# Two MLPs behind a retention attention: weights split in pairs, first weight loaded ahead of the chunks

## The chip, the cores and the metric

The kernel runs on one core of one Trainium2 chip. The metric is the device time of one execution in microseconds (us); less is better. It is the time of the whole program on that core, from the first load to the last store.

## The reference, cut to what matters

Four batches of 576 tokens (2304 in all) with 8 heads of 64 dimensions go through a retention attention, and then through two MLPs of 512 to 2048 to 512 columns, all in float32:

```python
scores = q @ k.T / sqrt(64);  D[i, j] = gamma[h] ** (i - j) if i >= j else 0
x = (scores * D) @ v                                  # per head, heads side by side: 2304 x 512
x = softplus(x @ w1_in) @ w1_out                      # first MLP, softplus = max(h, 0) + log1p(exp(-|h|))
out = relu(x @ w2_in) ** 2 @ w2_out                   # second MLP
```

The weights of both MLPs lie in memory as 64-bit floats, so a row of weights is loaded as pairs of 32-bit words.

## The kernel before

**Precision.** A float32 matrix product is made of three products of reduced-precision float32 (fp32r): each operand is split into a part `hi` (a rounding copy) and a part `lo` (the operand less `hi`), and hi*hi, lo*hi and hi*lo are summed in PSUM.

**Weights.** A weight tile is 128 x 512. `load_w` brings its 64-bit numbers (512 KB) into one of three staging slots (`STAGES = 3`) by the SP queue; the load of a slot's next owner waits until the slot has been read. `words` makes float32 of it: on ACT L140 (`Prelu`) and L141 (`Identity`), on DVE L145 (shift and or), which is the last to read the slot and writes `ct`. Then `split_w` makes `hi` on ACT (L173) and `lo` on DVE (L174). So a weight tile costs three operations of 128 x 512 on ACT and two on DVE. `items` is the order in which weights are split, `pump_step` does one part of the next item, `pump(n)` whole items; `weights(j)` says how many items are to be done by step j. There are 16 tiles of `wi` (first matrix) and 16 of `wo` (second) in each MLP.

**Opening.** The attention works on chunks of 64 tokens. `load_chunk(c)` loads q and k (`qk`, 256 KB) and k and v (`kv`, 256 KB) by SP; `scale_v(c)` (L311) multiplies v by decay factors; `step_s(c)` does 16 or 32 small matmuls (scores L326, state L332), masks the scores on DVE (L336) and copies the state on ACT (L338); `step_o(c)` does 16 matmuls into `po` (L348), makes `x` on DVE (L361), its hi part `xh` on ACT (L365) and its lo part `xl` on DVE (L366). `make_xw` (DVE, L710) prepares factors. The first eight chunks make the first tile of tokens; the code from `with tc.manual_schedule()` on writes the order on every engine by hand. `scale_v` runs there on POOL, but for chunk 7, which is done on DVE. `keep_warm` puts filler matmuls (`cold`, L684) between. `wi` 0 is loaded behind chunk 4, `wi` 1 and 2 behind chunk 7, and from chunk 5 on one `pump_step` follows each chunk.

**First MLP.** Tokens go in five tiles of 512, 384, 512, 512 and 384 (`TILES`), each in 16 steps f. Step j: `g1(j)`, 12 matmuls (L401) into one of two PSUM banks; `softplus_a` on ACT (L415 to L417), `split_g` of the step before (ACT L437, DVE L438); then the weights that are due (first tile only) and attention work for the next tile (`attend`); `g2(j - 2)`, 12 matmuls (L453); `softplus_b` on DVE (L422, L425, L428, which frees the bank). A scheduler decides how these interleave on each engine. The weights of the first MLP stay in SBUF, hence only the first tile splits weights.

**Second MLP.** It works by Strassen-like products (L545, seven for every block) and pieces (L564). Their left operands are sums of weight blocks that `split_s` makes during tiles 1 to 3 and stores in DRAM (`s2d`, read back into `S_SLOTS` slots); the right operands (`build_t`: ACT L533, DVE L534 on 768 columns) are built in the last tile of the first MLP, in buffers that the first MLP's `wi` leaves. The last tile and the first block also split the second MLP's `wo`.

## Time and profile before

| | us |
|---|---|
| median of three executions | 874.39 (874.03 to 876.84) |
| the profiled execution | 873.48 |
| its span, first to last instruction | 871.7 |
| PE busy | 858.3 |
| DVE busy | 579.7 |
| ACT busy | 422.2 |

The profile is of one execution. Its time is 1.78 us above its span (what lies around the first and the last instruction). PE is TensorE's matmuls, PEld its weight loads, DVE is VectorE, ACT is ScalarE, POOL is GpSimd, SP is SyncE, which here only issues DMAs. A row of a timeline gives start, duration, engine, line and operation, `out<-in`, shapes, and in brackets how long the engine had been idle before and what ended that.

### The profile page before, as it was taken

Reading aid. Unit: us, or ns where it says so; the run is one execution under the profiler, and the core shown is the slowest. Engines: PE = TensorE matmul, PEld = TensorE weight load, DVE = VectorE, ACT = ScalarE, POOL = GpSimd, SP = SyncE. Lnnn points to the kernel's source line nnn. Section 1 sums busy time; section 2 is a strip of 40 time slices with the busy share of each in tenths; the row PEclk is TensorE's granted clock in tenths of the full one; section 3 lists DMA queues with packets and bytes.
Section 4 is the critical chain, followed back from the end, with each engine's and each line's share of the span. In section 5 each row is a group of like instructions: output and inputs, shape, how many; then the busy total and the mean of one; then the engine's idle time right before and its main releaser. Section 6 shows DMA issues by size and latency. Waiting matters only on the chain.

```text
span 871.7 us, 14212 instructions
## 1 busy us (share of the span) xinstructions
PE 858.3 (98%) x5520; PEld 754.4 (87%) x5520; DVE 579.7 (67%) x1002; ACT 422.2 (48%) x763; POOL 8.8 (1%) x12
## 2 busy tenths in 40 slices
PE   8899999999999999999999999999999999999998
PEld 7777888999888888888999989888888988998896
DVE  3799899977896578745788874447645446553544
ACT  2599997665675446644696561213322113221121
POOL 2100000000000000000000000000000000000000
PEclk9999999999999999999999999999999999999999
DMA  9867764861583117610432464436644343644442
GB/s 209 229 181 211 220 210 148 246 203 50 165 264 104 30 45 239 221 36 1 170 115 55 149 226 121 120 110 193 193 115 115 121 118 115 191 120 115 116 121 85
DMA packets 75766, 126.32 MB, mean 145 GB/s; under 512 B 6706, under 2 KB 41650, under 8 KB 75698
## 3 DMA queue, kind: packets, MB, share of 16 engines
q1 hardware_dynamic: 75700, 125.42, 48.7%
q8 instruction: 44, 0.72, 0.3%
q14 instruction: 22, 0.18, 0.1%
HBM read 101.28 MB, written 24.12 MB: 144 GB/s over the span
## 4 chain that ended last, share of the span: by engine, by line
PE 83%; DMA 6%; DVE 4%; ACT 4%; issue 1%; SPq 0%; POOL 0%; DVEq 0%; ACTq 0%
PE acc L564 23%; PE acc L453 18%; PE ph L401 18%; PE py L545 9%; PE px L545 6%; PE pz L545 6%; PE st L326 2%; DMA wo_raw<-in_moe_w_out_dram 2%; DMA ch<-in_kv_dram 2%; PE po L348 2%; DMA wi_raw<-in_moe_w_in_dram 1%; DVE ct L145 1%; PE st L332 1%; DMA ch<-in_qk_t_dram 1%; ACT e L416 1%
## 5 line engine op out<-in xcount | busy, mean ns | idle before, releaser
L401 PE MATMUL ph<-xh,wi 128*128 128x512 f32 (+1 forms) x640 | 146.2, 369 | 2.9 <-DVE e L428 2.1
L401 PEld LDWEIGHTS ph<-xh,wi 128*128 128x128 f32 x640 | 116.3, 188 | 19.9 <-DVE e L428 2.2
L453 PE MATMUL acc<-gh,woh 128*128 128x512 f32 (+1 forms) x320 | 120.5, 378 | 0.0
L453 PE MATMUL acc<-gl,woh 128*128 128x512 f32 (+1 forms) x320 | 117.8, 368 | 0.2 <-DVE gl L438 0.2
L453 PE MATMUL acc<-gh,wol 128*128 128x512 f32 (+1 forms) x320 | 117.8, 368 | 0.0
L564 PE MATMUL acc<-woh,gring 128*128 128x512 f32 x288 | 104.9, 393 | 0.0
L545 PE MATMUL py<-t,sring 128*128 128x384 f32 x432 | 86.9, 335 | 0.3 <-DVE uring L652 0.3
L545 PEld LDWEIGHTS py<-t,sring 128*128 128x128 f32 x432 | 77.2, 188 | 6.8 <-DVE uring L652 0.6
L437 ACT CAST gh<-e 128x512 fp32r<-128x512 f32 (+1 forms) x80 | 45.8, 573 | 71.6 <-DVE e L428 54.2
L401 PE MATMUL ph<-xl,wi 128*128 128x512 f32 (+1 forms) x320 | 78.7, 367 | 0.0
L422 DVE SCALAR_TENSOR_TENSOR e<-e 128x512 f32<-128x512 f32 (+1 forms) x80 | 50.9, 636 | 38.0 <-ACT l L417 37.2
L438 DVE TENSOR_TENSOR gl<-e,gh 128x512 fp32r<-128x512 f32 (+1 forms) x80 | 50.9, 636 | 29.1 <-ACT gh L437 28.6
L453 PEld LDWEIGHTS acc<-gh,woh 128*128 128x128 f32 x320 | 60.0, 188 | 8.9 <-ACT gh L437 0.2
L453 PEld LDWEIGHTS acc<-gh,wol 128*128 128x128 f32 x320 | 60.1, 188 | 7.9
L590 ACT CAST gh<-g 128x384 fp32r<-128x384 f32 x48 | 24.6, 513 | 86.8 <-DVE g L577 72.1
L453 PEld LDWEIGHTS acc<-gl,woh 128*128 128x128 f32 x320 | 60.1, 188 | 7.5 <-DVE gl L438 0.4
L401 PEld LDWEIGHTS ph<-xl,wi 128*128 128x128 f32 x320 | 58.7, 188 | 7.6
L590 ACT CAST gring<-g 128x384 fp32r<-128x384 f32 x48 | 24.6, 513 | 83.0 <-DVE g L577 83.0
L415 ACT ACTIVATE e<-ph 128x512 f32<-128x512 f32 (+1 forms) x80 | 44.0, 550 | 37.3 <-PE ph L401 37.1
L564 PEld LDWEIGHTS acc<-woh,gring 128*128 128x128 f32 x288 | 54.0, 188 | 9.2
L545 PE MATMUL px<-t,sring 128*128 128x384 f32 x288 | 58.3, 337 | 0.0
L545 PE MATMUL pz<-t,sring 128*128 128x384 f32 x288 | 58.2, 337 | 0.0
(82 smaller groups left out, 1497.1 us busy)
## 6 DMA issues: line engine op xcount, KB each, us to landing
sring<-s2d SPq DMA_DIRECT2D x168, 256.0 KB, 2.7
wi_raw<-in_moe_w_in_dram SPq DMA_DIRECT2D x32, 512.0 KB, 4.6
wo_raw<-in_moe_w_out_dram SPq DMA_DIRECT2D x32, 512.0 KB, 4.2
s2d<-ct SPq DMA_DIRECT2D x48, 256.0 KB, 3.0
ch<-in_qk_t_dram SPq DMA_DIRECT2D x36, 256.0 KB, 4.3
ch<-in_kv_dram SPq DMA_DIRECT2D x36, 256.0 KB, 4.9
raw<-x2d SPq DMA_DIRECT2D x12, 384.0 KB, 3.3
out_dram<-xo SPq DMA_DIRECT2D x18, 256.0 KB, 2.2
```

The source lines that it names most:

```text
L145: nc.vector.scalar_tensor_tensor(out=ct, in0=up, scalar=3, in1=low, op0=ALU.logical_shift_left, op1=ALU.bitwise_or,)
L326: nc.tensor.matmul(pb[HI, h, :], lhsT=kk[LO, h, :], rhs=qp[LO, h, :], start=True, stop=True, skip_group_check=True,)
L348: nc.tensor.matmul(po[(LO, HI)[h % 2], h // 2, :], lhsT=sv[rows, h, :], rhs=qp[rows, h, :], start=True, stop=True, skip_group_check=True,)
L401: nc.tensor.matmul(ph[:, :n], lhsT=a, rhs=x, start=(j == 0), stop=(j == len(todo) - 1))
L415: nc.scalar.activation(out=e, in_=ph[:, :n], func=AF.Abs)
L422: nc.vector.scalar_tensor_tensor(out=e, in0=e, scalar=-2.0, in1=e, op0=ALU.add, op1=ALU.mult)
L437: nc.scalar.copy(h[:, :n], g)
L438: nc.vector.tensor_tensor(out=l[:, :n], in0=g, in1=h[:, :n], op=ALU.subtract)
L453: nc.tensor.matmul(acc[j][:, :n], lhsT=a, rhs=x, start=(begin and m == 0), stop=(end and m == 2))
L545: nc.tensor.matmul(ps, lhsT=a, rhs=x, start=(first and m == 0), stop=(m == len(todo) - 1), skip_group_check=True,)
L564: nc.tensor.matmul(acc2[j, m], lhsT=a, rhs=x, start=(begin and n == 0), stop=(end and n == 2))
L590: nc.scalar.copy(h, g)
```

## The change

**Pairs.** Weights are split in pairs of tiles. The words of the two tiles are still made one by one (L140, L141, L145), each into one half of a `ct` of 2 x 512 columns; then one ACT copy (L172 of the changed file) and one DVE subtraction (L173) work on 1024 columns. `wi` 0 and `wi` 1 stay single. After each tile's words one further load is asked for. The order of items becomes `wi` 0, `wi` 1, `wi` 2-3, `wo` 0-1, `wi` 4-5, `wo` 2-3 and so on; `weights(j)` counts pairs. `split_s` and the stores of its results use pair buffers too, but keep their operations.

**Buffers.** `cvt` has three slots of 2 x 512 columns in place of six of 512. `wi` tiles lie in groups of six in place of three, `wo` in pairs; `build_t` uses such a group for four results, and runs in steps 7 to 10 and 13 to 15 of the last tile (before: 4, 5, 7, 8, 10, 11, 13), and the last tile splits a pair in steps 4, 7, 10 and 13 (before: one tile in every even step from 4). `S_SLOTS` goes from 5 to 4.

**Opening.** The load of `wi` 0 is the first behind the two rows of constants; one `pump_step` follows each of chunks 0 to 2 (before: 5 to 7). All `scale_v` are on POOL; 12 fillers in place of 4 stand ahead of chunk 0; `make_xw(8)` comes last.

```diff
-EARLY = {"wi": 9, "wo": 8}
-GROUP = 3
+EARLY = {"wi": 12, "wo": 8}
+GROUP = 6
...
-S_SLOTS = 5
+S_SLOTS = 4
...
-    cvt = ctx.enter_context(tc.tile_pool(name="cvt", bufs=6))
+    cvt = ctx.enter_context(tc.tile_pool(name="cvt", bufs=3))
...
-        return cvt.tile([P, DM], dtype, tag="ct", name="ct")
+        return cvt.tile([P, 2, DM], dtype, tag="ct", name="ct")
...
-    def split_w(phase, kind, f):
-
-        t = staged.pop((kind, f))
-        ct = new_ct()
-        yield from words(t, ct)
+    def split_w(i, n, phase, kind, f):
+
+        ct = new_ct()[:, :n]
+        for o in range(n):
+            yield from words(staged.pop(i + o), ct[:, o])
+            pump_load(i + o + 1 + STAGES)
         y = ct.bitcast(F32)
...
+        w = wi_group[phase, kind, g][:, m:m + n]
+        hi, lo = w[:, :, 0], w[:, :, 1]
         nc.scalar.copy(hi, y)
         nc.vector.tensor_tensor(out=lo, in0=y, in1=hi, op=ALU.subtract)
...
+    want(1, split_w, (0, "wi", 0), (w1_in, "wi", 0))
+    want(1, split_w, (0, "wi", 1), (w1_in, "wi", 1))
+    for f in range(2, KF + 2, 2):
         if f < KF:
-            items.append((1, split_w, (0, "wi", f)))
-            loads.append((w1_in, "wi", f))
-        if f >= 2:
-            items.append((1, split_w, (0, "wo", f - 2)))
-            loads.append((w1_out, "wo", f - 2))
+            want(2, split_w, (0, "wi", f), (w1_in, "wi", f), (w1_in, "wi", f + 1))
+        want(2, split_w, (0, "wo", f - 2), (w1_out, "wo", f - 2), (w1_out, "wo", f - 1))
...
-                    if b == 0 and k in (0, 3):
-                        if n_split[0] < len(items) and not (p >= 4 and k == 3):
-                            pump(1)
+                    if b == 0 and k == 0 and n_split[0] < len(items):
+                        pump(1)
...
+        pump_load(1)
         load_chunk(0)
         nc.sync.dma_start(out=cst[:, :C_XW], in_=consts[:, :C_XW])
         for c in range(1, last + 1):
             load_chunk(c)
-            if c == last - 4:
-                pump_load(1)
-            elif c == last - 1:
+            if c == last - 1:
                 pump_load(3)
...
-        keep_warm(4)
+        keep_warm(12)
         for c in range(last + 1):
-            scale_v(c, nc.vector if c == last - 1 else nc.gpsimd)
+            scale_v(c, nc.gpsimd)
             if c < last:
                 keep_warm(1)
                 step_s(c, True)
                 if c:
                     step_o(c - 1, ps_acc)
-                make_xw(c + 1)
-                if c >= last - 3:
+                if c + 1 < last:
+                    make_xw(c + 1)
+                if c < 3:
                     pump_step()
         keep_warm(2)
         step_o(last - 1, ps_acc)
+        make_xw(last)
         keep_warm(6)
...
-        first = (2, 2, 2, 3)[:j + 1]
-        return min(n_one, 2 + int(sum(first) + 1.9 * (j + 1 - len(first))))
+        return min(n_one, 3 + j + (j > 0))
...
-            if f >= 4 and f % 2 == 0:
+            if f in (4, 7, 10, 13):
                 pump(1)
-            for i in range(7):
-                if f == GROUP * (i // 2) + GROUP + 1 + i % 2:
-                    build_t(i)
+            if GROUP < f <= GROUP + 4:
+                build_t(f - GROUP - 1)
+            elif f > 2 * GROUP:
+                build_t(f - 2 * GROUP + 3)
```

Three places in the order of instructions follow. The first is ACT at the end of the opening. `wi_raw` is a staged weight (L140 with a wait on a DMA is the first to touch it), `L365` (changed: `L364`) casts one chunk's `xh`. Before, the last `xh`, that of chunk 7, is the last row here:

```order
L140 ACTIVATE wi_raw<-wi_raw 128x512 [waits DMAHW5_49]
L365 CAST xh<-x 128x4x64 [waits DVE_49]
L173 CAST wi_439<-ct 128x512
L141 ACTIVATE wi_raw<-wi_raw,cst 128x512
L365 CAST xh<-x 128x4x64 [waits DVE_49]
```

With the change the same stretch reads, with `xh` of chunk 6 in the second row and of chunk 7 in the sixth:

```order
L141 ACTIVATE wi_raw<-wi_raw,cst 128x512
L364 CAST xh<-x 128x4x64 [waits DVE_49]
L140 ACTIVATE wi_raw<-wi_raw 128x512 [waits DMAHW5_49]
L172 CAST wi_274<-ct 128x512 [waits DVE_49]
L141 ACTIVATE wi_raw<-wi_raw,cst 128x512
L364 CAST xh<-x 128x4x64 [waits DVE_49]
L140 ACTIVATE wi_raw<-wi_raw 128x512 [waits DMAHW0_49,Activation_49]
L414 ACTIVATE e<-ph 128x512 [waits PE_49]
```

In both, the first L140 shown is that of `wi` 2. What stands ahead of it moved: `wi` 0 is long done, the weight whose copy stands here (L172) is `wi` 1, and the next L140 (`wi` 3) stands ahead of the first softplus (L414).

The second place is the loads on SP, in the opening. `L120` is a load of a `wi` tile, `L125` of a `wo` tile, `L296` and `L300` are the two halves of a chunk. Before, behind `wi` 1 and 2:

```order
L120 DMA wi_raw<-in_moe_w_in_dram 128x4x256 x2
L297 DMA ch<-in_qk_t_dram 64x1024
L301 DMA ch<-in_kv_dram 64x1024
L125 DMA wo_raw<-in_moe_w_out_dram 128x1024
L297 DMA ch<-in_qk_t_dram 64x1024
```

The changed kernel starts with `wi` 0 and goes on behind chunk 7 (rows 20 to 23 of SP) as follows:

```order
1 L717 DMA rows_in<-in_consts_dram 1x2304 x2
2 L120 DMA wi_raw<-in_moe_w_in_dram 128x4x256
3 L296 DMA ch<-in_qk_t_dram 64x1024
4 L300 DMA ch<-in_kv_dram 64x1024
5 L722 DMA cst<-in_consts_dram 128x138
...
20 L120 DMA wi_raw<-in_moe_w_in_dram 128x4x256 x2
21 L296 DMA ch<-in_qk_t_dram 64x1024
22 L300 DMA ch<-in_kv_dram 64x1024
23 L120 DMA wi_raw<-in_moe_w_in_dram 128x4x256
```

The bytes ahead of chunks 5 to 8 and of `wi` 1 and 2 are the same as before; those ahead of chunks 0 to 4 grew by one weight. Behind chunk 8 the next load is `wi` 3 (before `wo` 0), and `wo` 0 and 1 come behind chunks 9 and 10.

The third place is DVE between the first g1 and the third, in the changed kernel; L421, L424 and L427 are `softplus_b` of step 0, L310 scales chunks 9 and 10, L335 masks chunk 9, L173 is the `lo` part of the pair `wi` 2-3:

```order
L145 SCALAR_TENSOR_TENSOR ct<-wi_raw 128x512 [waits DMAHW0_49,Activation_49]
L421 SCALAR_TENSOR_TENSOR e<-e 128x512 [waits Activation_49]
L310 TENSOR_TENSOR ch<-ch,cst 64x512 [waits DMAHW2_49]
L173 TENSOR_TENSOR wi_274<-ct,wi_274 128x2x512 [waits Activation_49]
L424 SCALAR_TENSOR_TENSOR l<-e,l 128x512 [waits DVE_49]
L335 TENSOR_TENSOR ch<-st,cst 64x512 [waits PE_49]
L310 TENSOR_TENSOR ch<-ch,cst 64x512 [waits DMAHW4_49]
L427 SCALAR_TENSOR_TENSOR e<-ph,l 128x512 [waits DVE_49]
```

Before, the scaling of chunk 9 stood ahead of the first L422, and a `lo` part of 512 columns between them; the rest of the sequence was the same.

## Rows read from the trace of the kernel before

**Rows 1.** The page, part 1: busy time, share of the span, instructions.
```profile
span 871.7 us, 14212 instructions
...
PE 858.3 (98%) x5520; PEld 754.4 (87%) x5520; DVE 579.7 (67%) x1002; ACT 422.2 (48%) x763; POOL 8.8 (1%) x12
```

**Rows 2.** Windows of the opening: length, then busy time (count) of each engine, PEclk, DMA.
```profile
10.00:15.00 5.00, 4.99 (x115) 4.41 (x116) 3.18 (x7) 1.93 (x4) 2.09 (x2) 1.00 1.03 223
...
20.00:25.00 5.00, 4.63 (x64) 3.98 (x62) 2.60 (x5) 1.38 (x3) 2.09 (x2) 0.50 1.04 248
...
17.00:18.00 1.00, 0.00 (x0) 0.00 (x0) 0.53 (x3) 0.40 (x1) 0.00 (x0) 1.00 1.00 208
...
19.00:20.00 1.00, 1.00 (x26) 0.88 (x23) 0.33 (x1) 0.18 (x1) 0.00 (x0) 0.62 1.08 234
```

**Rows 3.** Timeline of POOL: start, us, line, operation, idle before.
```profile
15.71 1.05 POOL L311 TENSOR_TENSOR ch<-ch,cst 64x512 f32<-64x512 f32 x1 [1.22 <-DMA ch<-in_kv_dram]
21.23 1.04 POOL L311 TENSOR_TENSOR ch<-ch,cst 64x512 f32<-64x512 f32 x1 [4.48 <-DMA ch<-in_kv_dram]
```

**Rows 4.** Timelines of DVE and ACT, 29 to 43 us.
```profile
29.50 0.69 DVE L145 SCALAR_TENSOR_TENSOR ct<-wi_raw 128x512 uint32<-128x512 uint32 x1
30.21 0.69 DVE L311 TENSOR_TENSOR ch<-ch,cst 64x512 f32<-64x512 f32 x1
...
42.43 0.69 DVE L422 SCALAR_TENSOR_TENSOR e<-e 128x512 f32<-128x512 f32 x1
...
33.16 0.71 ACT L140 ACTIVATE wi_raw<-wi_raw 128x512 f32<-128x512 f32 x1
33.75 0.40 ACT L365 CAST xh<-x 128x256 fp32r<-128x256 f32 x1
34.04 0.62 ACT L173 CAST wi<-ct 128x512 fp32r<-128x512 f32 x1
34.56 0.79 ACT L141 ACTIVATE wi_raw<-wi_raw,cst 128x512 uint32<-128x512 uint16 x1
```

**Rows 5.** Timeline of PE, 31 to 56 us.
```profile
31.00 0.24 PE L332 MATMUL st<-ch 64*64 64x64 f32 x1 [2.50 <-ACT wi_raw L141]
...
32.05 0.69 PE L348 MATMUL po<-ch 128*64 128x64 f32 x16
...
36.52 2.11 PE L401 MATMUL ph<-xh,wi 128*128 128x512 f32 x8
...
46.06 2.10 PE L401 MATMUL ph<-xh,wi 128*128 128x512 f32 x8
...
52.34 1.98 PE L401 MATMUL ph<-xh,wi 128*128 128x512 f32 x8
...
55.06 0.39 PE L453 MATMUL acc<-gh,woh 128*128 128x512 f32 x1
```

**Rows 6.** DMA issues at 14.55 and at 18.76 us: last column us to landing.
```profile
ch<-in_kv_dram SPq DMA_DIRECT2D x1, 256.0 KB, 10.9
...
wi_raw<-in_moe_w_in_dram SPq DMA_DIRECT2D x1, 512.0 KB, 11.3
```

**Rows 7.** Windows of the first tile.
```profile
36.52:46.06 9.54, 9.47 (x110) 7.21 (x108) 8.42 (x14) 5.89 (x11) 0.00 (x0) 1.00 0.91 236
46.06:134.60 88.54, 86.86 (x547) 70.13 (x545) 81.45 (x134) 85.78 (x153) 0.00 (x0) 1.00 0.67 198
```

**Rows 8.** Groups by line, whole run: count, busy us, mean ns, idle before.
```profile
L534 DVE TENSOR_TENSOR t<-raw,t 128x768 fp32r<-128x768 f32 x21 | 20.1, 957 | 6.2 <-ACT t L533 5.9
...
L173 ACT CAST woh<-ct 128x512 fp32r<-128x512 f32 x32 | 19.7, 615 | 3.2 <-DVE ct L145 2.7 <-PE acc L453 0.2
...
L533 ACT CAST t<-raw 128x768 fp32r<-128x768 f32 x21 | 17.4, 830 | 8.0 <-PE px L545 3.2 <-PE pz L545 2.6 <-PE py L545 2.3
```

**Rows 9.** Waits of PE, 46 to 135 us and 425 to 480 us: total, times, longest.
```profile
PE ph L401 <- DVE e L428: 0.9, 1, 0.9
...
PE ph L401 <- DVE e L428: 1.2, 3, 0.5
```

More of the change, by code (lines that the diff above doesn't have):

```diff
@@ L151, in new_ct @@
     def new_ct(dtype=U32):
[L152 removed]
+        return cvt.tile([P, 2, DM], dtype, tag="ct", name="ct")
     wi_group = {}
[L156 to L160 removed]
+    def split_w(i, n, phase, kind, f):
[3 more added lines that the diff above has]
+            pump_load(i + o + 1 + STAGES)
         y = ct.bitcast(F32)
         pool = wts if f < EARLY[kind] else late_wts[0]
[L163 to L172 removed]
+        g, m = divmod(f, GROUP if kind == "wi" else 2)
+        if (phase, kind, g) not in wi_group:
+            size = min(GROUP, KF - g * GROUP) if kind == "wi" else 2
+            wi_group[phase, kind, g] = pool.tile(
+                [P, size, 2, DM], F32R, tag=f"{kind}{g}", name=f"{kind}{g}"
+            )
+        w = wi_group[phase, kind, g][:, m:m + n]
+        hi, lo = w[:, :, 0], w[:, :, 1]
         nc.scalar.copy(hi, y)
         nc.vector.tensor_tensor(out=lo, in0=y, in1=hi, op=ALU.subtract)
[L175 removed]
+        for o in range(n):
+            w_hi[phase, kind, f + o], w_lo[phase, kind, f + o] = hi[:, o], lo[:, o]
         yield True
@@ L180, in store_s @@
         n = src.shape[1] // (KH * P)
-        h, l = (new_ct(F32R)[:, :n * KH * P] for _ in range(2))
+        o = new_ct(F32R)
+        h, l = (o[:, part, :n * KH * P] for part in range(2))
         nc.scalar.copy(h, src)
@@ L188, in store_s, with split_s @@
             )
-    def split_s(p):
-        cts = []
-        for f in (p, p + NP):
-            t = staged.pop(("wi", f))
-            cts.append(new_ct())
-            yield from words(t, cts[-1])
-        top, bot = (ct.bitcast(F32) for ct in cts)
+    def split_s(i, n, p):
+        ct = new_ct()
+        for o in range(n):
+            yield from words(staged.pop(i + o), ct[:, o])
+            pump_load(i + o + 1 + STAGES)
+        top, bot = (ct[:, o].bitcast(F32) for o in range(2))
         a11, a12 = top[:, :KH * P], top[:, KH * P:]
@@ L252, in pump_step @@
                 return
-            count, make, args = items[m]
-            pump_load(n_used[0] + count)
-            splitting.append(make(*args))
+            i, n, make, args = items[m]
+            pump_load(i + n)
+            splitting.append(make(i, n, *args))
             n_split[0] += 1
-            n_used[0] += count
+            n_used[0] += n
         if next(splitting[0]):
@@ L479, in second_buffers @@
         mem["s"] = xs.tile([P, 4, 2, KH * P], F32R, tag="xr", name="sring")
-        mem["s4"] = cvt.tile([P, 2, KH * P], F32R, tag="ct", name="sring")
     def raw(i, j):
```

45 lines of the change are left out of this document (15 added, 30 removed).

## The prediction

> **What bounds the kernel now.** The page's first part comes first: PE is busy 858.3 of 871.7 us [rows 1], so outside the opening there is little to win but PE's own work, which the change leaves as it is. What PE loses it loses before the first g1, which starts at 36.52 [rows 5]; everything behind shifts with it. So the second view is the opening by windows, and there three things are to be seen.
>
> First, POOL waits 4.48 us for chunk 5, which arrives for its 21.23 scaling while the one before ran at 15.71 [rows 3]: one weight, `wi` 0, was loaded between them. [...] Third, PE stands 2.50 us ahead of 31.00, in the state matmuls of chunk 7 [rows 5]. The row names an ACT operation on `wi_raw`, but what these matmuls need is the scaled v, and DVE does that scaling at 30.21, behind the joining of `wi` 0's words at 29.50 [rows 4]. Chunk 7 itself had landed at 14.55 + 10.9 = 25.45 [rows 6].
>
> The third view is the first tile. From 46.06 to 134.60 ACT is busy 85.78 of 88.54 us, PE 86.86 [rows 7]: ACT is nearly a second bound there, because it splits the weights. PE's waits in it are one of 0.9 us on DVE's last softplus operation and, in the last tile, 1.2 us in three [rows 9].
>
> **The opening, step by step.** With `wi` 0 ahead of everything, chunks 0 to 4 come later by one weight's transfer, and from chunk 5 on the same bytes lie ahead as before; so I keep 25.45 for chunk 7, and 18.76 + 11.3 = 30.06 for `wi` 2 [rows 6]. The gap between chunks 4 and 5 is gone, and with it, I hold, the half clock. `wi` 0's words are split early and are behind nobody at the end. So chunk 7: POOL scales it in 1.04 [rows 3], to 26.5; 32 small matmuls take 31.00 to 32.05, so 1.05, to 27.6 [rows 5]; the mask, an operation of 0.69 as the DVE rows of 512 columns are [rows 4], to 28.3; `po` 0.69 [rows 5], to 29.0. On DVE `x` and `xl` of chunk 6 and the words of `wi` 1 stand ahead of `x` of chunk 7, about 0.42 + 0.69 + 0.42 (0.42 is 0.69 less 0.27 for 256 columns, as worked out below), so `x` is ready at about 30.2.
>
> That is not what decides. On ACT the cast `xh` of chunk 7 now stands behind L140 of `wi` 2, L172 of `wi` 1 and L141 of `wi` 2, and L140 waits for the landing at 30.06. Those rows in before follow each other as 33.16, 33.75, 34.04, 34.56 with durations 0.71, 0.40, 0.62, 0.79 [rows 4]: the start-to-start times are 0.59 for L140 and 0.52 for the copy, about 0.69 for L141, then 0.40 of the cast itself. 30.06 + 0.59 + 0.52 + 0.69 + 0.40 = 32.26. The first g1 starts at 32.3 instead of 36.52: **4.2 us earlier**. If that block of ACT did not stand there it would be 30.2 + 0.4 = 30.6; every us that `wi` 2 comes later costs one.
>
> **From the first g1 to the third.** Before, 46.06 - 36.52 = 9.54 [rows 5]. Now DVE and ACT set it. g1 takes 55.06 - 52.34 = 2.72 [rows 5], to 35.0. ACT's three softplus operations with L141 of `wi` 3 between them are four that follow each other by 0.52 to 0.69 as above, to about 37.5. Then DVE does, one behind the other, L421 (0.69 as at 42.43), scaling of chunk 9 (0.69 as at 30.21) [rows 4], the pair's `lo` (1.15, below), L424 and the mask of chunk 9 (0.69 each); with some 0.07 of overlap in each of the five, that is 37.5 + 3.9 - 0.35 = 41.05. `po` (0.69) and the next chunk's matmuls (1.05) follow on PE, to 42.8, or with hand-overs 43.1. So the third g1 begins at about 43.1 instead of 46.06: of 4.2 us **2.9 are left** and 1.3 are lost to the pair and the chunk that now fall into this place. Bounds: 0 to 2.4 lost, the upper one if the chunk's scaling also waits for its landing by half of the 2.27 (1.22 + 1.05) at which chunks follow each other [rows 3].
>
> **The pairs.** No row shows a copy or a subtraction of 1024 columns. ACT copies 512 in 0.615 and 768 in 0.830, DVE subtracts 768 in 0.957 [rows 8] and does 512 in 0.69 [rows 4]. 256 columns more cost 0.215 and 0.267, so 1024 columns are estimated at 1.045 and 1.22: a pair costs 0.185 less on ACT and 0.16 less on DVE than two single ones. But consecutive single operations overlap by about 0.1 (33.16 + 0.71 against 33.75 [rows 4]), which leaves 0.08 for each pair in time of the queue. With 15 pairs in the first tile that is 1.2 us on ACT and about as much on DVE. Bounds: 0, if 1024 columns cost two times 512; 15 x 0.4 = 6 us of ACT, if they cost no more than 768. I take the value in line with the two widths shown. None of it is PE's time, since PE is the longer one in that stretch by 86.86 to 85.78 [rows 7]; it is cover for what the change adds there: a pair's first tile waits for the second, a third of the step's weights comes earlier (four tiles of words in step 1 against two), and ACT is occupied for 1.05 us at a stretch. I let the one pay for the other: **0**, with the two sides below as rivals. The eight pairs of the second MLP save 8 x 0.08 on ACT and DVE, which are not what PE waits for there: 0, or 0.5 either way if a burst of two tiles' words falls ahead of a product, the size of the longest of the three waits in the last tile [rows 9].
>
> **The rest.** `build_t` keeps its count of operations, in fewer steps but next to fewer splits; the waits that it is near, 1.2 us in three, and the 0.9 in the first tile [rows 9] can each go or come back. I give a gain of **0.4** of these 2.1, bounds -0.5 and +2.1. The smaller cache of `s2d` slots, the new groups of `wi` buffers and the drain in a whole pair slot I cost at nothing: PE has four products of work in hand for a load, and the drains fall where ACT is less than half busy over the run (422.2 of 871.7 [rows 1]). If that cover is gone, it is 0.5 again.
>
> **Sum.** 2.9 + 0 + 0.4 = 3.3 us off the profiled execution: 873.48 - 3.3 = 870.2. That execution lies 0.91 below the median of 874.39, so the median forecast is 871.1.
>
> **Rivals.**
>
> *The clock falls again.* With `wi` 0 first, PE waits for chunk 0 by one weight's transfer more, and the 12 fillers in place of 4 may not reach. Idle time of about 1 us at 17 to 18 was enough ahead of the fall to 0.50 [rows 2]. While it lasted, PE did 64/115 of its work; a chunk is then 2.27 x 115/64 = 4.1 us instead of 2.27 [rows 3], and in a spell of the same length (19 to 25 at least) two to three chunks fall 4 to 5 us back. Chunk 7 has about 1.7 us in hand (30.6 against 32.3), so g1 is late by some 3, of which the DVE chain gives back 1.3: gain 3.3 - 1.7 = 1.6, median 872.8. For it: the waits between chunks stay. Against: at 10 to 15 the same feed of a chunk each 2.27 us kept PE 4.99 of 5.00 busy at 1.00 [rows 2]. [...]
>
> *The lead is eaten.* PE cannot use a lead if ACT is the bound: 2.76 us idle in 88.54 [rows 7] is less than the 2.9 of lead plus the words that come earlier. Then the first waits for `wo` 0-1 and the pairs behind it take it all, and 0.4 or less is left: 874.0. Against: the pairs give 1.2 us back, and ACT can start with the words earlier too.
>
> *Pairs stall PE at each step (slower).* An ACT queue that is 97% busy lets the next softplus start later by what a copy is longer, 1.045 - 0.615 = 0.43, and PE, which has two banks for g1, stands for it: 15 x 0.43 = 6.5 us, less 3.3: 877.6. It turns to slower from 0.22 us of stall for each pair on. For it: 85.78 of 88.54. Against: in before a `lo` part and words lay in the same place and PE waited once.
>
> *All of the lead stays.* If the third g1 follows its 9.54 as before and the waits of 2.1 go by half: 4.2 + 1.0 = 5.2, median 869.2. For it: scaling of chunk 9 in before also stood there.
>
> **How the numbers follow.** Forecast (869.9 to 872.3) 0.42; all of the lead (868.4 to 869.9) 0.15; clock 0.10; lead eaten (872.3 to 874.8) 0.20; slower 0.13. A measurement of this kernel tells 0.3%, 2.6 us, from no change, so faster is below 871.8 and slower above 877.0. Faster: 0.15 + some 0.36 of the forecast's 0.42 + 0.02 of the others = 0.53. Slower: 0.13 and 0.01 of worse mishaps = 0.14. Same: the rest, 0.33. The range 868.4 to 874.8 leaves out the slower case and a little at the low end.
>
> **What would show it.** In the changed profile: POOL's scalings 2.3 us apart with no gap at chunk 5, PEclk at 1.00 from 15 to 30 us; the last `xh` behind `wi` 2's landing near 30.1 and the first L400 at 32.3; the third g1 near 43.1 behind DVE; pair copies near 1.05 and subtractions near 1.22; PE's waits in the first tile below 2 us in all. Wrong it is if the first L400 starts after 34 (clock, or `wi` 2 late), if L400 or L452 wait on ACT or DVE step by step up to 130 us, or if the last tile's waits grow by more than 1 us.

## The result, and the profile after

| | before | changed |
|---|---|---|
| median, four executions each, same chip (us) | 874.61 (874.03 to 876.84) | 881.65 (880.03 to 882.32) |
| ratio, 95% interval | | 1.0063 [1.0043, 1.0082] |
| the profiled execution (us) | 873.48 | 882.08 |
| its span | 871.7 | 880.3 |

The change makes the kernel slower by 0.6%. The forecast was 871.1 with a range of 868.4 to 874.8; the measured 881.65 lies well above it. One caution for all that follows: beside the experiments the kernel before ran 104 times, in four batches with medians of 876.0 to 876.5, and only two of the 104 were faster than the profiled 873.48. Of the 8.6 us between the two profiles, the ratio vouches for 4 to 7 (0.43 to 0.82%). One execution of all, the profiled one of `e14` (1895 us), was disturbed and is left out of every number below.

The page of the changed kernel, part 1, against [rows 1]:

```profile
span 880.3 us, 14194 instructions
...
PE 862.7 (98%) x5536; PEld 755.7 (86%) x5536; DVE 579.5 (66%) x978; ACT 419.4 (48%) x740; POOL 10.4 (1%) x13
```

ACT has 23 operations less, one for each of the 15 + 8 pairs, and 2.8 us less busy time. PE has 16 more matmuls (fillers) and is busy 4.4 us longer. Windows of its opening (length, busy time and count of each engine, PEclk, DMA), against [rows 2]:

```profile
15.00:20.00 5.00, 2.78 (x56) 2.24 (x54) 4.43 (x8) 2.08 (x4) 2.59 (x2) 1.00 1.04 231
20.00:25.00 5.00, 4.55 (x68) 3.90 (x70) 2.67 (x6) 1.39 (x3) 2.09 (x2) 0.68 1.05 249
...
35.00:40.00 5.00, 2.65 (x17) 2.16 (x16) 2.02 (x5) 0.91 (x3) 0.00 (x0) 0.88 0.72 161
40.00:45.00 5.00, 5.00 (x31) 3.49 (x30) 1.28 (x3) 2.36 (x4) 0.00 (x0) 0.77 0.38 111
```

PE lost nearly half of two windows, 15 to 20 and 35 to 40, and behind each the granted clock fell (0.50 from 21.77 to 25.19 and from 38.84 to 42.25 in finer windows, 1.00 before and behind; 0.50 is called half clock below). The timeline of PE says what the two losses were, against [rows 5]:

```profile
20.45 0.57 PE L347 MATMUL po<-ch 128*64 128x64 f32 x12 [2.33 <-issue]
...
37.35 0.68 PE L325 MATMUL st<-ch 64*64 64x64 f32 x9 [2.35 <-issue]
37.96 3.06 PE L400 MATMUL ph<-xh,wi 128*128 128x512 f32 x8
...
42.50 0.69 PE L347 MATMUL po<-ch 128*64 128x64 f32 x16
...
49.21 0.68 PE L347 MATMUL po<-ch 64*64 64x64 f32 x16 [1.44 <-DVE ch L335]
...
50.62 1.65 PE L400 MATMUL ph<-xh,wi 128*128 128x512 f32 x6
```

`[2.33 <-issue]` means that no semaphore, DMA or engine of the profile released PE: it stood in the middle of `po` of one chunk, with its operands there, and 2.33 us later went on with the same 16. The first g1 starts at 37.96 (forecast 32.3, before 36.52), takes 4.54 us to the `po` at 42.50 instead of 2.72 because it lies in the half clock, then `po` of chunk 9 waits 1.44 us for a mask (L335) on DVE, and the third g1 starts at 50.62 (forecast 43.1, before 46.06).

How far the changed kernel's profile is behind that of before, by the start of the n-th of the large matmuls (L400 and L452, which both kernels issue in the same order):

| n, where | before | changed | behind |
|---|---|---|---|
| 0, first g1 | 36.52 | 37.96 | 1.44 |
| 24, third g1 | 46.06 | 50.62 | 4.56 |
| 300, late in the first tile | 119.42 | 124.98 | 5.56 |
| 400, second tile | 145.67 | 154.62 | 8.95 |
| end of span | 871.69 | 880.30 | 8.61 |

So there are two large losses: some 4.6 us up to the third g1, and 3.4 at the end of the first tile; 1.0 goes between them. The last tile of the first MLP and what follows give 0.35 back.

### The profile page after: what moved, and what is told of

Read it like the earlier page. It is cut to its first block, busy times and chain, and to the rows that moved or that the text cites. A ratio compares the mean times of both kernels' runs of the same rounds, so it can differ in the third digit from the quotient of the medians.

```text
span 880.3 us, 14194 instructions
## 1 busy us (share of the span) xinstructions
PE 862.7 (98%) x5536; PEld 755.7 (86%) x5536; DVE 579.5 (66%) x978; ACT 419.4 (48%) x740; POOL 10.4 (1%) x13
## 4 chain that ended last, share of the span: by engine, by line
PE 87%; ACT 4%; DMA 3%; DVE 3%; issue 1%; SPq 1%; POOL 0%; DVEq 0%; ACTq 0%
PE acc L561 22%; PE ph L400 19%; PE acc L452 19%; PE py L542 9%; PE pz L542 6%; PE px L542 6%; PE st L325 3%; PE po L347 2%; DMA ch<-in_kv_dram 2%; DMA wo_raw<-in_moe_w_out_dram 1%; PE st L331 1%; ACT l L416 1%; DVE ct L145 1%; ACT wo L172 1%; DMA wi_raw<-in_moe_w_in_dram 1%
## 5 line engine op out<-in xcount | busy, mean ns | idle before, releaser
L452 PE MATMUL acc<-gh,wo 128*128 128x512 f32 (+1 forms) x640 | 200.1, 373 | 0.0
L400 PE MATMUL ph<-xh,wi 128*128 128x512 f32 (+1 forms) x640 | 148.2, 372 | 3.7 <-DVE e L427 3.3
L400 PEld LDWEIGHTS ph<-xh,wi 128*128 128x128 f32 x640 | 116.4, 188 | 21.4 <-DVE e L427 5.0
L452 PEld LDWEIGHTS acc<-gh,wo 128*128 128x128 f32 x640 | 118.6, 188 | 17.5 <-ACT gh L436 0.7
L452 PE MATMUL acc<-gl,wo 128*128 128x512 f32 (+1 forms) x320 | 117.9, 368 | 0.9 <-DVE gl L437 0.9
L561 PE MATMUL acc<-wo,gring 128*128 128x512 f32 x432 | 114.9, 393 | 0.0
L561 PEld LDWEIGHTS acc<-wo,gring 128*128 128x128 f32 x432 | 80.0, 188 | 12.7
L561 PE MATMUL acc<-wo,gh 128*128 128x512 f32 x288 | 90.0, 393 | 0.0
L400 PE MATMUL ph<-xl,wi 128*128 128x512 f32 (+1 forms) x320 | 79.7, 370 | 0.0
L421 DVE SCALAR_TENSOR_TENSOR e<-e 128x512 f32<-128x512 f32 (+1 forms) x80 | 51.0, 637 | 38.5 <-ACT l L416 38.0
L452 PEld LDWEIGHTS acc<-gl,wo 128*128 128x128 f32 x320 | 60.1, 188 | 8.2 <-DVE gl L437 1.4
L400 PEld LDWEIGHTS ph<-xl,wi 128*128 128x128 f32 x320 | 59.3, 190 | 8.1 <-DVE xl L383 0.2
L414 ACT ACTIVATE e<-ph 128x512 f32<-128x512 f32 (+1 forms) x80 | 44.2, 552 | 42.5 <-PE ph L400 41.9
L561 PE MATMUL acc<-wo,gl 128*128 128x512 f32 x144 | 57.2, 397 | 0.0
```

What stands on the lines that cost most here:

```text
L400: nc.tensor.matmul(ph[:, :n], lhsT=a, rhs=x, start=(j == 0), stop=(j == len(todo) - 1))
L414: nc.scalar.activation(out=e, in_=ph[:, :n], func=AF.Abs)
L421: nc.vector.scalar_tensor_tensor(out=e, in0=e, scalar=-2.0, in1=e, op0=ALU.add, op1=ALU.mult)
L452: nc.tensor.matmul(acc[j][:, :n], lhsT=a, rhs=x, start=(begin and m == 0), stop=(end and m == 2))
L561: nc.tensor.matmul(acc2[j, m], lhsT=a, rhs=x, start=(begin and n == 0), stop=(end and n == 2))
```

## The experiments

Each has the kernel before beside it on the same chip; the ratio is to that. "Changed" is the changed kernel. Where an expectation speaks of PE's record 449, 705 or 961, it counts matmuls, weight loads and PE's few semaphore entries in one series (220 + 220 + 9 = 449).

### Which part: the pairs, the opening, or the fillers

Theory: the opening is slower by PE's stops for something that "issue" hides, and by the half clock behind them. Rivals: the pairs stall the first tile; the 12 fillers push PE into the stop.

`e1_pairs_only` is the changed kernel with the opening of before.

```diff
-        pump_load(1)
         load_chunk(0)
...
+            if c == last - 4:
+                pump_load(1)
...
-        keep_warm(12)
+        keep_warm(4)
...
-            scale_v(c, nc.gpsimd)
+            scale_v(c, nc.vector if c == last - 1 else nc.gpsimd)
...
-                if c < 3:
+                if c >= last - 3:
                     pump_step()
```

> The changed kernel with the opening of before (loads, fillers, scalings and the steps of the first weight as they were). Theory: the 8.6 us are two sums, 4.6 us lost by the third g1 (the opening) and 4.4 us lost between there and the end of the first tile (the pairs), with 0.4 given back in the last tile. By it the first g1 starts at 36.5 as before, PE waits some 3 us between 120 and 145 us, and the time is 878 to 879. Rival: the pairs only suffer from the late start of the weights in the opening; then the time is that of before, 874 to 875.

Measured: 882.23, ratio 1.0070 [1.0043, 1.0097]. The pairs alone are as slow as the whole change. The expected 878 to 879 with a first g1 at 36.5 did not come: in the profile the first g1 starts at 41.70, behind a stop of 2.85 us and two spells of half clock of 10.24 us each. A part of the ratio is therefore clock: the three executions at a mean granted clock of 0.994, the clock of before, took 880.3 to 880.5 (some 1.0045), the three at 0.986 to 0.992 took 884.0 to 885.9.

`e2_opening_only` is the reverse: the kernel before with the opening of the changed one (first weight ahead, 12 fillers, all scaling on POOL).

> The kernel before with the opening of the changed one. Theory: PE's code arrives in blocks of 256 records, at record 449, 705 and 961 counted over matmuls and weight loads, and the opening decides at which work these fall; this kernel has the same PE work there as the changed one, so PE stands still some 2.3 us at record 449 and again at record 961 with a fall of the clock behind each, the first g1 starts near 38 and the time is 878 to 880. Rival: the pairs' words and loads delay the end of the opening; then the first g1 starts at 32 to 34 and the time is 870 to 873.

Measured: 878.39, 1.0025 [1.0008, 1.0042]. The opening alone gains nothing either; its profile has stops of 2.37 and 0.70 us at the expected records 449 and 961, two spells of half clock in the opening, and the first g1 at 38.49.

`e3_fill4` is the changed kernel with four fillers.

```diff
-        keep_warm(12)
+        keep_warm(4)
```

> The changed kernel with 4 fillers ahead of chunk 0 in place of 12, which is 32 PE records fewer in front of everything. Theory of the code blocks: record 449 then falls into the scores of chunk 5 as before (idle 1.4 us, not 2.3) and record 961 into the first g1, where the queue is full of long matmuls, so the second stop and the second fall of the clock are gone, the first g1 starts at 34 to 35.5 and the time is 876 to 878. Rival: the late chunks behind the first weight's load make the idle time, and the fillers only cover it; then the time stays at 881 to 882 or grows.

Measured: 881.42, 1.0057 [1.0040, 1.0074]. Stops of 1.61 and 1.42 us (records 449 and 705) instead of 2.33 and 2.35, first g1 at 35.88, and the time the same, not the expected 876 to 878. The fillers are not it.

`e4_pair_order_single_ops` keeps loads, order, buffers and pairs, but makes each pair's copy and subtraction as two of 512 columns.

```diff
-        nc.scalar.copy(hi, y)
-        nc.vector.tensor_tensor(out=lo, in0=y, in1=hi, op=ALU.subtract)
+        for o in range(n):
+            nc.scalar.copy(hi[:, o], y[:, o])
+            nc.vector.tensor_tensor(
+                out=lo[:, o], in0=y[:, o], in1=hi[:, o], op=ALU.subtract
+            )
```

> The changed kernel with each pair's copy and subtraction done as two of 512 columns, order and loads as in the changed one. Theory: the 4.4 us in the first tile come from the order (two weights of one kind behind each other, their loads in bursts, ACT and DVE in order behind a load that has not landed), so they stay: 881 to 883. Rival: the long operations of 1.04 and 1.23 us hold up the softplus; then the time falls to 877 to 878.

Measured: 877.47, 1.0007 [0.9989, 1.0025]. With the shorter operations the loss is gone, where the theory of the order had 881 to 883. This run puts the slowdown on the wide operations, not on the order of loads, the buffers or the opening. One reserve: its mean granted clock was 0.9963, against 0.9933 and 0.9942 in `e5` and `e8` below. 0.0030 of 877 is 2.6 us, so by my estimate at most that much of the 4 to 5 us between them can be clock. `e9` and `e11` repeat the comparison further down with nearly equal clocks.

### Why a wide operation costs: its length, or what it waits for

A wide operation is longer, and it also cannot begin before both tiles' words are there. `e5_halves_across` separates them: two operations of 512 elements in a row as in e4, but each on one half of the columns of both tiles.

```diff
+        parts = [slice(0, DM)] if n == 1 else [slice(0, DM // 2), slice(DM // 2, DM)]
+        for c in parts:
+            nc.scalar.copy(hi[:, :, c], y[:, :, c])
+            nc.vector.tensor_tensor(
+                out=lo[:, :, c], in0=y[:, :, c], in1=hi[:, :, c], op=ALU.subtract
+            )
```

> The changed kernel with each pair's copy and subtraction cut in two the other way: each half takes 256 columns of both tiles, so each is as long as a single operation (512 columns) and still needs the words of both tiles. Theory of the dependence: what the pairs lose is that nothing of a pair can be copied before its second tile has landed and been joined, so this kernel is as slow as the changed one, 1.0055 to 1.008 of before. Theory of the length: 1.04 and 1.23 us operations hold up the softplus; then this kernel is as the one with two single operations, 1.000 to 1.003.

Measured: 881.19, 1.0056 [1.0035, 1.0078], as slow as the change. Its copies take 0.61 us and its subtractions 0.69, as those of e4 do. Same length as e4, same dependence as the change: it is the dependence.

`e6_single_ops_fill4` is e4 with four fillers.

> The changed kernel with two single operations for each pair and 4 fillers in place of 12 in the opening. If the fillers' 32 records only move the code blocks to a better place, 0.998 to 1.000 of before; if the opening of the changed kernel is as good with either, 1.001 as with 12.

Measured: 876.29, 1.0000 [0.9983, 1.0017], not clearly apart from e4.

`e7_first_weight_only` is the kernel before with only `pump_load(1)` ahead of chunk 0 and `pump_step` at `c < 3`.

> The kernel before with the first weight alone moved: its load first, its three steps behind chunks 0 to 2; fillers, scaling of chunk 7 on DVE and make_xw as before. My forecast's reason (late weight work out of the way of the last chunks) gives 0.995 to 0.997 of before. The theory of the code blocks gives no gain, since PE stops at record 449 and 705 for the arrival of code wherever the weight's load stands, and the clock falls behind it: 0.999 to 1.003.

Measured: 876.78, 1.0006 [0.9994, 1.0017]. To load the first weight first gains nothing by itself. Its profile has two stops (0.67 and 1.53 us) and the first g1 at 41.4, behind spells of half clock at 8.60 to 15.42 (after PE's wait of 2.24 us on POOL had begun) and 29.07 to 39.31 (from the end of the second stop).

`e8_changed_again` is the changed kernel unedited, to see which features of its profile repeat.

> The changed kernel itself once more, beside the others on the same chip, for its level there and a second profile. All theories: 1.005 to 1.008 of before; PE idle behind one or two of the records 449, 705 and 961, and a wait for a weight's landing late in the first tile.

Measured: 880.28, 1.0051 [1.0033, 1.0069]. One stop of 3.04 us, at the same instruction as the first of the changed profile; none at the other place. First g1 at 37.97.

### What the stops are, and what is left without them

The counts of PE's instructions at which it stops are the same in all nine kernels with eight chunk buffers, though few stop at all three. Windows from the start up to the inside of each stop, changed kernel (second and third number in brackets: matmuls and weight loads):

```profile
0.00:19.50 19.50, 15.73 (x220) 13.81 (x220) 7.27 (x14) 6.60 (x12) 5.92 (x9) 1.00 0.91 208
0.00:28.00 28.00, 22.88 (x345) 19.92 (x345) 12.55 (x25) 8.98 (x17) 9.31 (x12) 0.94 0.96 224
0.00:36.50 36.50, 29.80 (x471) 26.06 (x472) 18.66 (x36) 14.92 (x28) 10.36 (x13) 0.95 0.99 220
```

The same view of the kernel before, whose idle 17 to 18 stands in [rows 2], and of e1:

```profile
0.00:17.50 17.50, 15.18 (x219) 13.05 (x220) 6.48 (x15) 5.27 (x10) 5.42 (x9) 1.00 0.88 204
```

```profile
0.00:27.50 27.50, 23.67 (x345) 20.90 (x345) 10.96 (x24) 8.45 (x16) 7.50 (x11) 0.81 0.96 217
```

220 + 220, 345 + 345 and 471 + 472 instructions: about 250 to 253 apart, and 256 apart if PE's semaphore entries are counted too. The chunk that PE is at differs between the kernels, the count does not. What comes in at each of these places is a packet on a queue of its own. DMA view of the changed kernel, 17.7 to 17.8 us:

```profile
q8 instruction: 1, 0.02, 79.1%
```

It is one of 44 packets of 16 KB on that queue in the whole run, one for every 252 of PE's 11072 matmuls and weight loads, or every 257 with its semaphore entries: I take them for PE's code. PE enters a block, and the packet of the next one starts at (us):

| | PE enters block | packet of next block starts | PE goes on with the next |
|---|---|---|---|
| before | 10.6 | 15.66 | 18.34, stopped 1.43 |
| changed | 11.9 | 17.76 | 20.45, stopped 2.33 |
| changed | 28.1 | 34.58 | 37.35, stopped 2.35 |
| e9 (four chunk buffers, below) | 11.5 | 12.47 | 17.10, no stop |
| e9 | 17.1 | 17.59 | 25.26, no stop |

At the four stops in the profiles of before and changed (eight chunk buffers in both) PE goes on 2.47 to 2.77 us after the packet's start (the fourth is that of 0.49 us in the changed kernel: packet at 25.62, PE at 28.09). The packets of the first three of these blocks start 5.0, 5.9 and 7.3 us after PE has entered the block before in the kernel before, and 5.8, 5.2 and 6.5 in the changed one, while the loads that SP issues from 6 to 36 us land 6.6 to 13.7 us after their issue. The first of these blocks lasted 6.2 us in the changed kernel (11.9 to 18.1), less than the 5.8 us to its packet's start and the 2.7 behind it. Behind 50 us, with fewer loads under way (DMA 0.67 from 46.06 to 134.60 [rows 7], landings up to 135 us in 3.4 to 7.7 us) and larger matmuls, packets start from 4.5 us ahead of PE's entry into the block before to 2.1 us behind it, which is 9.5 us or more ahead of PE's going on with their own, and PE has no wait on "issue" there.

If queued loads delay the code, fewer chunk buffers should cure it, since a load then waits for a buffer and not in the queue. The next four kernels vary that.

```diff
-    first = tc.tile_pool(name="first", bufs=n_first)
+    first = tc.tile_pool(name="first", bufs=5)
```

(`n_first` is 8.) `e9_single_four_slots` and `e10_single_five_slots` are e4 with 4 and 5 buffers; `e11_changed_four_slots` and `e12_before_four_slots` are the changed kernel and the one before with 4.

> The changed kernel with two single operations for each pair, and with four chunk buffers in the opening in place of eight, so that a chunk's load is issued only when the chunk four before it is used up. Theory: PE asks for each block of code when it enters the one before, but in the opening the block's packet starts only 4 to 9 us after that, behind the loads that are already queued (they land 8 to 11 us after their issue); with fewer loads in the queue the packet starts 2 to 4 us after it, PE no longer stops at records 449 and 705, the clock stays at 1.00, the first g1 starts at 33 to 35 and the ratio to before is 0.995 to 0.998 (1.001 with eight buffers). Rival: the code arrives late whatever else is queued; then the stops stay, and the later loads only add to them: 1.001 to 1.006.

> The same with five chunk buffers: more chunks in the queue. If the queue delays the code, the stops lie between those of four and eight buffers, unless four hold back the chunks themselves, when five is the better one: 0.995 to 0.999. By the rival the same as with eight: 1.001.

> The changed kernel, pairs and all, with four chunk buffers in the opening. If the opening and the pairs add up, it keeps the pairs' loss and wins the opening: 1.001 to 1.004 of before, with the waits at the end of the first tile as in the changed one.

> The kernel before with four chunk buffers. If queued loads hold up PE's code, it too loses its stop at record 449 and the fall of the clock: 0.995 to 0.999 of before. By the rival 1.000 or more.

| | median | ratio | first g1 in the profile |
|---|---|---|---|
| e9 | 876.16 | 1.0003 [0.9988, 1.0018] | 34.74 |
| e10 | 875.28 | 0.9998 [0.9979, 1.0017] | 34.22 |
| e11 | 879.64 | 1.0043 [1.0028, 1.0059] | 35.04 |
| e12 | 875.41 | 1.0003 [0.9987, 1.0019] | 37.58 |

The stops go in all four (PE's waits on "issue" up to 36 us are none in e9 and 0.2 us in e10). In e9 and e10 the first g1 comes 1.8 and 2.3 us ahead of [rows 5]. Yet the time does not follow, and the 0.995 to 0.999 expected of e9, e10 and e12 did not come: at n = 300 e9 is 3.06 us and e10 1.00 us *behind* before's profile. The lead goes in the first tile (in e9 a spell of half clock at 72.76 to 76.17 takes part). In e12 PE waits for POOL instead (1.04, 1.71 and 1.04 us for the scaling of later chunks), and 2.51 us ahead of chunk 7's state matmuls; its first g1 is no earlier.

e11 and e9 differ in the pairs' operations alone, and neither stops for code: 879.64 against 876.16, 3.5 us. The mean granted clocks are 0.9971 and 0.9982, and 0.0011 of 877 is 1.0 us: by this estimate the clock explains at most that much. Where the time goes, in the profiles (us between the starts of large matmuls):

| | before | single operations in pair order (e4, e6, e9, e10) | wide operations, or e5's across both tiles (changed, e3, e5, e8, e11) |
|---|---|---|---|
| first to third g1 | 9.54 | 9.47 to 9.49 | 11.10 to 12.66 |
| n = 24 to 300 | 73.36 | 76.72 to 78.26 | 74.36 to 78.05 |
| n = 300 to 400 | 26.25 | 25.28 to 26.03 | 27.42 to 29.64 |

The first row is the clearest. In the kernels of the last column `po` of chunk 9 waits 1.44 to 1.51 us behind the pair's `lo` and the mask, and behind that wait e3, e5, e8 and e11 have a spell of half clock of 3.41 us. The four with single operations have none at this place. Rows of e8, PE and a window:

```profile
47.67 0.86 PE L347 MATMUL po<-ch 64*64 64x64 f32 x16 [1.44 <-DVE ch L335]
```

```profile
48.02:51.43 3.41, 3.41 (x36) 2.96 (x33) 3.38 (x7) 2.67 (x6) 0.00 (x0) 0.50 0.09 18
```

So a part of what the wide operations cost goes with the clock. The second row shows another cost: pair order is slower there than the order of before even with single operations.

Two kernels put the opening into the kernel *before*, with its single operations and its own order of weights: `e13_before_new_opening_five` is e2 with five buffers, `e14_first_weight_five` is e7 with five buffers and 12 fillers.

> The kernel before with the changed opening and five chunk buffers; weights one by one in the order of before. Theory A, the lead is lost to the order of the pairs: with the order of before in the first tile the lead of 2 to 3 us at the first g1 is kept to its end, 0.996 to 0.998 of before. Theory B, the lead is lost because ACT has no time to spare in the first tile whatever the order: 0.999 to 1.001, with new waits of PE on softplus or gl in the first tile.

> The kernel before with the first weight's load and steps ahead, 12 fillers and five chunk buffers, and the scaling of chunk 7 on DVE as before. By theory A 0.996 to 0.999; by theory B 0.999 to 1.001. If the scaling on DVE is what holds the end of the opening, PE stands 1 to 2.5 us ahead of chunk 7's state matmuls here and not in the other.

Measured: e13 875.99, 0.9986 [0.9964, 1.0009]; e14 874.99 over eleven executions, 0.9983 [0.9967, 0.9998]. e14 has no profile that can be read, so its question on the scaling is not answered there. e13's profile is the fastest here, a span of 869.1. Rows of its PE:

```profile
32.92 2.11 PE L401 MATMUL ph<-xh,wi 128*128 128x512 f32 x8
...
42.18 2.08 PE L401 MATMUL ph<-xh,wi 128*128 128x512 f32 x8 [1.00 <-DVE e L428]
```

That is nearly the opening of the forecast: first g1 at 32.92 (32.3), third at 42.18 (43.1), PEclk 1.00 in every window of 10 to 45 us, one stop of 0.83. But its twelve executions fall into two groups. Five are at 871.0 to 872.5, with a mean granted clock of 0.999 or 1.000. One is at 874.79 and six at 877.2 to 878.7, with 0.993 to 0.998. The same kernel was run three more times, with a profile of each, to meet one of the upper group.

> The kernel of e13 once more, one look with a profile. Its times fell into two groups, 871.0 to 872.5 and 877.2 to 878.7. Theory: the second group is the executions in which a block of PE's code comes late or the clock falls (first g1 at 35 to 38 in place of 32.9, or 1.5 to 2 us lost to a stretch at 0.50); rival: the first tile's waits on ACT and DVE differ, with the same opening.

> The kernel of e13, a second look. Theory: a time of 877 to 879 goes with late code or a fall of the clock, one of 871 to 872.5 with neither; rival: the opening is the same in both and the first tile's waits differ.

> The kernel of e13, a third look. Theory: a time of 877 to 879 goes with late code or a fall of the clock, one of 871 to 872.5 with neither; rival: the opening is the same in both and the first tile's waits differ.

Measured: 872.90, 871.69 and 875.89 (before beside them 876.59), first g1 at 33.74, 33.29 and 33.27, no half clock in any. The 875.89 lost its lead later: 3.1 us against before's profile between n = 300 and 380 (118 to 142 us). Waits of PE from 40 to 140 us (total, times, longest), e17 and then e13:

```profile
PE ph L401 <- DVE e L428: 3.6, 5, 1.4
PE acc L453 <- DVE gl L438: 1.1, 1, 1.1
```

```profile
PE ph L401 <- DVE e L428: 1.6, 3, 1.0
```

So the same opening was followed by other waits, as the rival has it, in one execution between the two groups. No profile of an execution at 877 to 879 was caught. In the timed ones the clock says where part of it can go: by my estimate 0.0043 less mean clock is at most 3.8 of the 6.5 us between the two groups. What sets the clock off in one execution and not in the next is open.

## Why the prediction was wrong, by its steps

Two steps failed. The opening was to win 4.2 us at the first g1; alone (e2) it made the kernel 0.25% slower, some 2 us. The pairs were to cost 1.3 us up to the third g1 and 0 behind it; they cost 3.5 to 5.

**The step that failed first: "The gap between chunks 4 and 5 is gone, and with it, I hold, the half clock."** POOL's wait for chunk 5 did shrink, from 4.48 us [rows 3] to 2.59 here and to 1.13, that of the other chunks, in e8, the same kernel. PE stopped all the same, in e8 for 3.04 us. POOL in the changed profile and in e8:

```profile
21.01 1.04 POOL L310 TENSOR_TENSOR ch<-ch,cst 64x512 f32<-64x512 f32 x1 [2.59 <-DMA ch<-in_kv_dram]
```

```profile
19.33 1.25 POOL L310 TENSOR_TENSOR ch<-ch,cst 64x512 f32<-64x512 f32 x1 [1.13 <-DMA ch<-in_kv_dram]
```

In the idle of 17 to 18 us [rows 2] I read a missing chunk, because POOL waited in the same stretch. The timeline of PE at its end, which I did not read, says otherwise. Kernel before:

```profile
18.34 0.21 PE L326 MATMUL pb<-ch 64*64 64x64 f32 x1 [1.43 <-issue]
```

This is the second score matmul of chunk 4; the first had run at 16.64, and the chunk had been scaled from 15.71 on for 1.05 us [rows 3], so data was at hand. It was the code. To load a weight first does nothing for that: the loads queued around the boundary are as many as before (eight issued and not landed at the packet's start, 15.66 and 17.76), and the code came as late (its packet 5.8 us after PE entered the block before, 5.0 in the kernel before). So the changed profile has stops of 2.33, 0.49 and 2.35 us for one of 1.43, and a fall of the clock behind each of the long ones. Over the timed executions the clock is about the same in both kernels, 0.995 to 0.996 in the four of the changed kernel (0.990 to 0.998 in e8's eight) against a median of 0.994 before. 0.006 of 872 is 5.2 us: by this estimate that is the most a full clock could have given, and the change did not get it.

The fall is the mechanism of the rival "the clock falls again", with another cause: in the changed profile the two spells follow the two stops of over 2 us, 1.3 and 1.5 us after PE goes on, and none follows the stop of 0.49. By my reading these were waits for code; in e11 a spell (21.50 to 24.91) follows a wait for data, of 1.24 us on POOL ahead of 19.94. A fall does not follow every stop: in e3's profile there is none behind those of 1.61 and 1.42 us, while in before's one followed 1.43.

One reading of the opening held. The wait of 2.50 us ahead of chunk 7's state matmuls [rows 5] is gone in every profile in which POOL scales chunk 7, and there in those that left it on DVE: 1.40 us in e7, 2.51 in e12, 2.73 in e1 (put down to "issue" there, but not at one of the counts above).

**First g1 at 32.3, "xh(7) behind wi2's landing".** `wi` 2 landed at 29.89, as estimated (30.06). It did not decide. ACT and DVE of the changed kernel:

```profile
32.53 0.41 ACT L364 CAST xh<-x 128x256 fp32r<-128x256 f32 x1 [0.15 <-DVE x L360]
32.84 0.68 ACT L140 ACTIVATE wi_raw<-wi_raw 128x512 f32<-128x512 f32 x1
33.77 0.62 ACT L172 CAST wi<-ct 128x512 fp32r<-128x512 f32 x1 [0.26 <-DVE ct L145]
34.30 0.77 ACT L141 ACTIVATE wi_raw<-wi_raw,cst 128x512 uint32<-128x512 uint16 x1
34.96 0.40 ACT L364 CAST xh<-x 128x256 fp32r<-128x256 f32 x1
...
32.41 1.33 DVE L145 SCALAR_TENSOR_TENSOR ct<-wi_raw 128x512 uint32<-128x512 uint32 x1
...
46.60 1.23 DVE L173 TENSOR_TENSOR wi<-ct,wi 128x1024 fp32r<-128x1024 f32 x1
```

L140 of `wi` 2 stands behind chunk 6's `xh`, which waits for `x` of a PE that the first stop made late. The block of L140, L172, L141 and `xh` is in the order and of the length forecast (2.5 us from 32.84 to 35.36; the sum had 2.2). Then the stop at 35.01 to 37.35 holds the last nine of chunk 8's sixteen score matmuls (L325), and g1 with them. Where the code comes nearly in time (stops of 0.36 to 1.07 us in e13 and its three further executions) g1 comes at 32.9 to 33.7, so the size of this step about stands; there too it is chunk 6's `x`, not the landing, that L140 stands behind.

**"1.3 of 4.2 lost" up to the third g1.** 12.66 us from first to third instead of the forecast 10.8. 1.82 of it is g1 at half clock (4.54 for 2.72). The DVE chain forecast, with the pair's `lo` between, is there: `lo` at 46.60 (1.23 long) holds L424 and the mask behind it, PE waits 1.44 us. (The sum had 1.15 for it, its own estimate 1.22.) With g1 at full clock the stretch took 11.1 to 11.6 us (e3, e5, e8, e11), and 9.5 with single operations. So some 2 us of what the pairs cost lie here, where the sum had 1.3: mis-sized, but the right mechanism.

**Pairs, 0.** All told the pairs cost 0.4 to 0.5%, 3.5 to 5 us. Less the 2 us at the third g1, this term, the rest of the first tile, failed by some 1.5 to 3. The durations were right. Groups of the changed kernel:

```profile
L173 DVE TENSOR_TENSOR wo<-ct,wo 128x1024 fp32r<-128x1024 f32 x16 | 19.6, 1223 | 4.1 <-ACT wo L172 4.1
...
L172 ACT CAST wo<-ct 128x1024 fp32r<-128x1024 f32 x16 | 16.8, 1048 | 0.3 <-DVE ct L145 0.3
```

1223 and 1048 ns, estimated 1.22 and 1.045. "A pair's first tile waits for the second" was named and then balanced against 0.08 us a pair. It is worth more, because ACT and DVE take their operations in the order in which the kernel has them (the ACT rows from 32.53 to 34.96 above stand in the order listed with the change, waits included). At the end of the first tile, changed kernel, ACT, DVE and PE:

```profile
126.42 0.67 ACT L140 ACTIVATE wo_raw<-wo_raw 128x512 f32<-128x512 f32 x1 [1.18 <-DMA wo_raw<-in_moe_w_out_dram]
127.00 0.74 ACT L141 ACTIVATE wo_raw<-wo_raw,cst 128x512 uint32<-128x512 uint16 x1
127.64 1.03 ACT L172 CAST wo<-ct 128x1024 fp32r<-128x1024 f32 x1
128.57 0.59 ACT L414 ACTIVATE e<-ph 128x512 f32<-128x512 f32 x1
...
127.77 0.69 DVE L145 SCALAR_TENSOR_TENSOR ct<-wo_raw 128x512 uint32<-128x512 uint32 x1 [1.10 <-ACT wo_raw L141]
128.49 0.69 DVE L427 SCALAR_TENSOR_TENSOR e<-ph,l 128x512 f32<-128x512 f32 x1
...
129.24 2.12 PE L400 MATMUL ph<-xh,wi 128*128 128x512 f32 x8 [1.38 <-DVE e L427]
```

A weight lands late; ACT waits 1.18 us for it and can copy nothing meanwhile, DVE waits 1.10 behind ACT, L427 (which frees a bank for g1) behind that, and PE stands 1.38. In e4, ACT at the corresponding place:

```profile
123.39 0.61 ACT L173 CAST wo<-ct 128x512 fp32r<-128x512 f32 x1
124.48 0.68 ACT L140 ACTIVATE wo_raw<-wo_raw 128x512 f32<-128x512 f32 x1 [0.47 <-DMA wo_raw<-in_moe_w_out_dram]
125.06 0.60 ACT L173 CAST wo<-ct 128x512 fp32r<-128x512 f32 x1
```

One copy falls ahead of the landing and one behind the wait, and only 0.47 us of it is left. PE's waits from 120 to 146 us are 1.6, 0.8 and 0.4 in the changed kernel, 0.8, 0.7 and 0.4 in e8, 0.9 and 0.5 in e5, and none in e4, e6, e9 and e10. That e4 and e5 differ in dependence alone makes the dependence shown as the cause. These rows are one place where it is seen, the third g1 is the other. How much of the 3.5 to 5 us belongs to each, and to the clock, is not shown: the order of single events differs from one execution to the next, and e17, with single operations in the order of before, waits 2.8 us in all in the same stretch. The prediction also counted PE's waits in the first tile too low: beside the 0.9 us there is one of 0.7 on ACT's L381, so PE had 1.6 us to spare and not 0.9.

**The rivals.** "Pairs stall PE at each step" had the sign, and at 877.6 the nearest time, but not the mechanism: e5's operations are short and it is as slow. "The lead is eaten" holds for e9 and e10, where a lead of 1.8 to 2.3 us is gone at 120 us in the order of pairs, while e13 with before's order keeps 2.6 of 3.6 in its profile (n = 24 to 300: 76.7 us or more in pair order, 74.6 in e13). As timed, e13 and e10 differ too little (0.9986 against 0.9998) to call that shown.

**The rest, 0.4.** The last tile gave 0.35. The span-to-time difference of 1.78 us was again 1.78.

No version here clearly beats the kernel before; the best, e14 at 0.9983 [0.9967, 0.9998], lies within the 0.3% that stands for no change.

## What to carry to other kernels

Idle time put down to "issue" was here a wait of its own kind (0.49 to 3.04 us at the same counts): count the instructions up to it, and if the count is the same in other kernels, look at the code queue and at how many loads are queued beside it, before moving any data. Joining two tiles in one operation saved an estimated 0.08 us of queue time a pair and makes it wait for the later of both; with ACT and DVE taking their operations in order behind late loads (ACT waited 1.18 us for one, PE 1.38 behind it) this cost 0.2 to 0.3 us a pair here (3.5 to 5 us over 15), three to four times the saving. And one profile is one execution: the one of before was 2.5 to 3 us under that kernel's median in the four batches beside the experiments, so a sum made against it starts with that error.

## What was not expected of the hardware

- PE's code (so I read the packets of queue 8) arrives late in a stretch full of loads: stops of 0.49 to 3.04 us at the same instruction counts in nine kernels, gone with four or five chunk buffers instead of eight in e9, e10, e11 and e12, and 0.36 to 1.07 us in the four profiles of e13's kernel.
- The DVE operation L145 at 32.41 of the changed kernel took 1.33 us instead of 0.69, while POOL scaled a chunk from 32.14 to 33.19. It ended 0.55 after POOL did. Other operations of its profile and of before's show the like: `xl` (256 columns, 0.42 alone) took 1.29 us at 17.41 (changed) beside POOL's scaling of 17.38 to 18.42, and 0.78 at 21.78 in the kernel before beside that of 21.23 to 22.28; both ended 0.28 after POOL. Three of POOL's scalings took 1.26 us (before, at 31.27), 1.54 and 1.30 (changed, at 15.12 and 25.39) instead of 1.04: there L145 or, at 25.37, `make_xw` had started first, and POOL ended 0.90 us after it.
- The same program, e13, on the same chip has executions at 871 and at 878 us that the mean granted clock tells apart (0.999 to 1.000, and 0.993 to 0.998).
